# Folding the quadrants of softmax row sums on GpSimd instead of with a matmul

## The chip, the cores and the metric

The kernel runs on one core of a Trainium2 chip. The metric is the time of one execution in device microseconds. Three to eleven executions of a kernel are timed, beside executions of the kernel before on the same chip; those of one kernel agree within some 0.5%. The engines are PE (TensorE matmul), PEld (its weight loads), DVE (VectorE), ACT (ScalarE), POOL (GpSimd) and SP (the engine that issues most DMAs).

## The reference, cut to what matters

Two independent problems A and B of the same shape are solved, and the results are concatenated. The softmax's denominator is the sum over 512 keys for each query and head.

```python
B, Sq, D = 16, 32, 1024
Hq, Hkv, Sk, Dh = 32, 4, 512, 128
q = (x @ wq).reshape(B, Sq, Hq, Dh).transpose(0, 2, 1, 3)
scores = einsum("bhqd,bhkd->bhqk", q, repeat(k)) * Dh ** -0.5
p = softmax(scores)
o = einsum("bhqk,bhkd->bhqd", p, repeat(v))
out = o.transpose(0, 2, 1, 3).reshape(B, Sq, Hq * Dh) @ wo
```

## The kernel before

The main part is a sequence of 128 slots. A slot handles one pair of batch and key head, that is 8 query heads of 32 queries. In slot i PE computes the scores of i (4 matmuls of 256 columns), ACT takes the exponential, DVE sums the probabilities (`partial_sums`), and PE computes the values of slot i - 4 (`LAG = GRP`, 4 matmuls of 256 columns). Between these PE runs six or seven "units", each one 512-column matmul of the query or output projections, so that it always has work.

The keys lie on the partitions, so the row sums have to cross partitions. DVE's reduction with a transpose leaves, in each 32-partition quadrant, the sums of that quadrant's keys. Once in four slots the chunks are added on DVE (`chunk_sums`), the four quadrants are added and spread by one float32r matmul with a constant 0/1 matrix (`fold_sums`), and DVE takes the reciprocal. `spread` widens two slots' reciprocals and `normalize` multiplies them onto the values.

```python
fold = const.tile([P, P // QD, QD], FP32R, name="fold")   # 0/1 matrix, filled by four casts
...
def fold_sums(k):
    cs = quad[k]
    sums = quad[k] = psum.tile([P, GRP * REP], FP32, name="sums", tag="sums", bufs=1)
    nc.tensor.matmul(sums[:], lhsT=fold[...], rhs=cs[...], start=True, stop=True)

def reciprocals(k):
    nc.vector.reciprocal(out=rall[:, k, :], in_=quad.pop(k)[:])
...
ob[j] = psum.tile([P, 2, QW], FP32, name="ob", tag="ob", bufs=1)   # values of two slots, ONE buffer
...
total_slots = 2 * NG                      # 128
LAG = GRP                                 # 4
for i in range(total_slots + LAG):
    live = i < total_slots
    k, o = divmod(i, GRP)
    j, odd = divmod(i - LAG, 2)
    folds = k >= 1 and k <= total_slots // GRP
    if live:
        do_loads(i)
        scores(i)
    run(units, 1)
    if o == 0 and folds:
        chunk_sums(k - 1)
    if i >= LAG:
        values(i - LAG)
    if o == 1 and folds:
        reciprocals(k - 1)
        spread(2 * k - 2)
    if o == 3 and folds:
        spread(2 * k - 1)
    if odd and j >= 0:
        normalize(j)
    run(units, 5)
    if o == 0 and folds:
        fold_sums(k - 1)
    if live:
        partial_sums(i)
    run(units, 1 - (i % 4 == 3))
```

Of the kernel before, what the change touches and what calls it, by code (L numbers as in the profile page):

```python
# [8 lines left out]
BF16 = mybir.dt.bfloat16  # L9
FP32 = mybir.dt.float32  # L10
FP32R = mybir.dt.float32r
I32 = mybir.dt.int32
ACTF = mybir.ActivationFunctionType
ALU = mybir.AluOpType
AX = mybir.AxisListType

P = 128
# [3 lines left out]
REP = HQ // HKV  # L21
QD = 32
# [151 lines left out]
def kernel(  # L174
# [14 lines left out]
    nc = tc.nc  # L189
    B, SQ, D = A_x.shape  # L190
# [3 lines left out]
    KC = SK // P  # L194
    TT = NTOK // P
    NOUT = D
    NW = 512
    NH = NOUT // NW
    GRP = 4
    NG = B * HKV  # L200
    BPT = P // SQ
    QW = REP * SQ
# [7 lines left out]
    def fast_path(ok_i):  # L210
        with ExitStack() as fctx:
            enter = fctx.enter_context
            const = enter(tc.tile_pool(name="const", bufs=1))
            blk = enter(tc.tile_pool(name="blk", bufs=20))
            kv = enter(tc.tile_pool(name="kv", bufs=3))
            work = enter(tc.tile_pool(name="work", bufs=2))
            outp = enter(tc.tile_pool(name="outp", bufs=2))
            psum = enter(tc.tile_pool(name="psum", bufs=2, space=bass.MemoryType.PSUM))
# [7 lines left out]
            nc.scalar.preload_act_table_set("natural_log_exp_and_others")  # L226


            warm = work.tile([P, NW], BF16, name="warm", tag="p_sb", bufs=6)
            nc.vector.memset(warm[:], 0.0)  # L230
            ident = const.tile([P, P], BF16, name="ident")
            make_identity(nc, ident[:])
            fold = const.tile([P, P // QD, QD], FP32R, name="fold")
            for r in range(P // QD):
                rs = slice(r * QD, (r + 1) * QD)
                nc.vector.tensor_copy(
                    out=fold[rs],
                    in_=ident[rs, rs].unsqueeze(1).to_broadcast([QD, P // QD, QD]),
                )
            one_col = const.tile([P, 1], FP32, name="one_col")  # L240
            nc.vector.memset(one_col[:], 1.0)
            shift = const.tile([P, 1], FP32, name="shift")
# [105 lines left out]
            def run(units, n):  # L348
                for _ in range(n):
                    next(units, None)  # L350


            def where(i):
                pr, ii = divmod(i, NG)
                if pr == 0:
                    g, b = divmod(ii, B)
                else:
                    b, g = divmod(ii, HKV)
                return pr, b, g
# [3 lines left out]
            def scores(i):  # L363
                pr, b, g = where(i)
                kT = k_tiles[i // GRP].rearrange("p q (k c) -> p q c k", c=KC)
                s_ps = psum.tile([P, KC, QW], FP32, name="s_ps", tag="s")
                for c in range(KC):
                    nc.tensor.matmul(  # L368
                        s_ps[:, c, :],
                        lhsT=kT[:, i % GRP, c, :],  # L370
                        rhs=qT[pr, g][:, b, :, :].rearrange("p h s -> p (h s)"),
                        start=True,
                        stop=True,
                    )
                p_sb = work.tile([P, KC, QW], BF16, name="p_sb", bufs=6)
                nc.scalar.activation(  # L376
                    out=p_sb[:], in_=s_ps[:], func=ACTF.Exp, bias=shift[:], scale=SCALE
                )
                st[i] = {"p": p_sb}

            parts, rcp, quad = {}, {}, {}

            def partial_sums(i):
                k, q = divmod(i, GRP)
                if q == 0:
                    parts[k] = work.tile([P, GRP, KC, REP], FP32, name="parts", bufs=1)
                nc.vector.tensor_reduce(  # L387
                    out=parts[k][:, q, :, :].rearrange("p c h -> p (c h)"),
                    in_=st[i]["p"][:].rearrange("p c (h s) -> p (c h) s", s=SQ),
                    axis=AX.X, op=ALU.add, apply_transpose=True,  # L390
                )

            def chunk_sums(k):
                cs = quad[k] = work.tile([P, GRP, REP], FP32R, name="cs", bufs=1)
                with nc.allow_low_precision(reason="float32r holds the float32 sum"):
                    nc.vector.tensor_reduce(  # L396
                        out=cs[:], in_=parts.pop(k)[:].rearrange("p q c h -> p q h c"),
                        axis=AX.X, op=ALU.add,
                    )

            def fold_sums(k):
                cs = quad[k]
                sums = quad[k] = psum.tile([P, GRP * REP], FP32, name="sums", tag="sums", bufs=1)
                nc.tensor.matmul(  # L404
                    sums[:],
                    lhsT=fold[:].rearrange("p r s -> p (r s)"),
                    rhs=cs[:].rearrange("p q h -> p (q h)"),
                    start=True,
                    stop=True,
                )  # L410

            def reciprocals(k):
                nc.vector.reciprocal(out=rall[:, k, :], in_=quad.pop(k)[:])  # L413

            def spread(j):
                k, o = divmod(j, 2)
                r = rcp[j] = work.tile([P, 2 * REP, SQ], FP32, name="r")
                nc.vector.transpose(  # L418
                    out=r[:].rearrange("p n s -> p (n s)"),
                    in_=rall[:, k, o * 2 * REP:(o + 1) * 2 * REP]  # L420
                    .unsqueeze(2).to_broadcast([P, 2 * REP, SQ]),
                )
# [3 lines left out]
            def values(i):  # L426
                v_sb = v_tiles[i // GRP]
                j, q = divmod(i, 2)
                if q == 0:
                    ob[j] = psum.tile([P, 2, QW], FP32, name="ob", tag="ob", bufs=1)  # L430
                for c in range(KC):
                    nc.tensor.matmul(  # L432
                        ob[j][:, q, :],
                        lhsT=v_sb[:, i % GRP, c, :],
                        rhs=st[i]["p"][:, c, :],
                        start=(c == 0),
                        stop=(c == KC - 1),
                    )

            def normalize(j):  # L440
                for i in (2 * j, 2 * j + 1):
                    normalized.add(where(i))
                    st.pop(i)
                pr, b, g = where(2 * j)
                tt, bl = divmod(b, BPT)
                if (pr, tt) not in oT:
                    oT[pr, tt] = blk_tile([P, HQ, P], "oT")
                if pr == 0:
                    out = oT[pr, tt][:, g * REP:(g + 1) * REP, bl * SQ:(bl + 2) * SQ]
                    out = out.rearrange("p h (q s) -> p q h s", s=SQ)  # L450
                else:
                    out = oT[pr, tt][:, g * REP:(g + 2) * REP, bl * SQ:(bl + 1) * SQ]
                    out = out.rearrange("p (q h) s -> p q h s", h=REP)
                nc.vector.tensor_tensor(  # L454
                    out=out,
                    in0=rcp.pop(j)[:].rearrange("p (q h) s -> p q h s", h=REP),
                    in1=ob.pop(j)[:].rearrange("p q (h s) -> p q h s", s=SQ),
                    op=ALU.mult,
                )
# [79 lines left out]
            for h, copy in enumerate((nc.vector.tensor_copy, nc.scalar.copy)):  # L539
                copy(  # L540
                    out=qT[0, 0][:, :, h, :],
                    in_=first_q[h][:].rearrange("p (b s) -> p b s", s=SQ),
# [44 lines left out]
            def do_loads(i):  # L587
                for fn, args in plan.get(i, []):
                    fn(*args)


            total_slots = 2 * NG
            LAG = GRP
            for i in range(total_slots + LAG):
                live = i < total_slots
                k, o = divmod(i, GRP)
# [5 lines that stand above are left out]
                run(units, 1)  # L602
                if o == 0 and folds:
                    chunk_sums(k - 1)
                if i >= LAG:
                    values(i - LAG)
                if o == 1 and folds:
# [4 lines that stand above are left out]
                if odd and j >= 0:  # L612
                    normalize(j)
                run(units, 5)
                if o == 0 and folds:
                    fold_sums(k - 1)
                if live:
                    partial_sums(i)
                run(units, 1 - (i % 4 == 3))
# [5 lines left out]
            for k, (lim, op) in enumerate(((1.0 / SUM_HI, ALU.is_ge), (1.0 / SUM_LO, ALU.is_le))):  # L625
                nc.vector.tensor_scalar(
                    out=sq[:], in0=rall[0:QD].rearrange("p j n -> p (j n)"),
# [48 lines left out]
```

## Time and profile before

| before | |
|---|---|
| time, median of 3 | 348.47 us |
| span of the profiled execution | 346.7 us |
| busy PE / DVE / ACT / POOL | 98% / 77% / 54% / 3% |
| chain that ended last | PE 98% |

From the page of the kernel before, part 1 (busy time and share of each engine) and two lines of part 5 (groups: line, engine, operation, output<-inputs, count, then busy us, mean ns of one, and the idle time in front with what ended it):

```profile
PE 341.1 (98%) x2185; PEld 218.4 (63%) x2185; DVE 265.8 (77%) x340; ACT 188.9 (54%) x213; POOL 8.9 (3%) x21
...
L404 PE MATMUL sums<-cs,fold 128*128 128x32 f32 x32 | 11.7, 367 | 0.0
L413 DVE RECIPROCAL rall<-sums 128x32 f32<-128x32 f32 x32 | 10.3, 320 | 0.5 <-PE sums L404 0.5
```

PE is the limit, and the other engines work in its shadow. The fold group, L404, looks like 11.7 us of PE. It is not: the spans of matmuls overlap. The 512-column ones of L312 have a mean span of 379 ns, and six of them below start within 72.25 - 70.96 = 1.29 us, 215 ns apart. The honest price is the distance between starts. The timeline of PE alone (columns: start us, us, engine, line, operation) shows a slot with a fold and the slot after it without one; a slot begins with its score matmuls `s_ps`:

```profile
67.44 0.60 PE L368 MATMUL s_ps<-qT,kT 128*128 128x256 bf16 x4
...
68.53 1.24 PE L312 MATMUL q_ps<-xT,wq_sb 128*128 128x512 bf16 x5
69.42 0.37 PE L404 MATMUL sums<-cs,fold 128*128 128x32 f32 x1
69.64 0.39 PE L312 MATMUL q_ps<-xT,wq_sb 128*128 128x512 bf16 x1
69.87 0.60 PE L368 MATMUL s_ps<-qT,kT 128*128 128x256 bf16 x4
...
70.96 1.46 PE L312 MATMUL q_ps<-xT,wq_sb 128*128 128x512 bf16 x6
72.25 0.60 PE L368 MATMUL s_ps<-qT,kT 128*128 128x256 bf16 x4
```

Both slots hold the same eight 256-column matmuls and seven 512-column ones. The one with the fold takes 69.87 - 67.44 = 2.43 us, the other 72.25 - 69.87 = 2.38 us. So a fold costs about 0.05 us in its place between wide matmuls.

### The profile page before, as it was taken

The page shows a single profiled execution, that of the slowest core. Times are in us where ns is not written, and L with a number is a line of the kernel's source. Part 1 is how long each engine was busy: PE and PEld are TensorE (multiplying, and loading weights), DVE is VectorE, ACT ScalarE, POOL GpSimd, SP SyncE. Part 2 cuts the span into 40 slices and gives each one's busy share as a digit, 9 for nine tenths or more (in the row PEclk, how much of TensorE's full clock was granted, in tenths as well). Part 3 has the DMA queues.
Part 4 walks back from the last instruction along what each step waited for, and adds up shares of the span by engine and source line. Part 5 has one row for each costly group of instructions (what it writes and reads, how often), then busy time and mean ns, then how long its engine had stood idle before and what let it go on. Part 6 is the DMA issues. An engine that isn't in the chain of part 4 may idle for free.

```text
span 346.7 us, 5462 instructions
## 1 busy us (share of the span) xinstructions
PE 341.1 (98%) x2185; PEld 218.4 (63%) x2185; DVE 265.8 (77%) x340; ACT 188.9 (54%) x213; POOL 8.9 (3%) x21
## 2 busy tenths in 40 slices
PE   8999999999999999999999999999999999999995
PEld 5656666666666666666666666666666666666554
DVE  2117888888888888888888888888988888888610
ACT  2357666666666766666655445555455545555000
POOL 0000000000000000000000000000000000000010
PEclk9999999999999999999999999999999999999998
DMA  7999999999986989999998449995669984410000
GB/s 226 247 311 338 164 274 277 242 256 275 247 242 166 209 238 223 297 274 267 278 310 207 110 125 288 351 257 121 137 196 286 301 200 118 112 36 2 15 33 19
DMA packets 125068, 71.70 MB, mean 207 GB/s; under 512 B 73616, under 2 KB 124048, under 8 KB 125040
## 3 DMA queue, kind: packets, MB, share of 16 engines
q1 hardware_dynamic: 124176, 69.29, 80.0%
q0 software_dynamic: 720, 1.97, 1.6%
q8 instruction: 18, 0.29, 0.3%
q14 instruction: 10, 0.08, 0.1%
q10 hardware_dynamic: 144, 0.07, 0.1%
HBM read 51.38 MB, written 2.10 MB: 154 GB/s over the span
## 4 chain that ended last, share of the span: by engine, by line
PE 98%; ACT 0%; issue 0%; DVE 0%; DVEq 0%; ACTq 0%
PE f_ps L331 32%; PE q_ps L312 31%; PE s_ps L368 16%; PE ob L432 16%; PE q_ps L517 1%; PE warm_ps L492 1%; PE xT_ps L507 1%; PE sums L404 0%; ACT o_sb L340 0%; DVE warm L230 0%; PE ok_ps L634 0%; DVEq L671 0%; ACTq L340 0%
## 5 line engine op out<-in xcount | busy, mean ns | idle before, releaser
L376 ACT ACTIVATE p_sb<-s_ps,shift 128x1024 bf16<-128x1024 f32 x128 | 142.5, 1114 | 101.7 <-PE s_ps L368 81.4
L387 DVE TRANSPOSE_TENSOR_REDUCE parts<-p_sb 128x32 f32<-128x1024 bf16 x128 | 158.9, 1241 | 45.5 <-ACT p_sb L376 45.4
L331 PE MATMUL f_ps<-wo_sb,oT 128*128 128x512 bf16 (+1 forms) x544 | 132.5, 367 | 0.0
L312 PE MATMUL q_ps<-xT,wq_sb 128*128 128x512 bf16 x496 | 128.8, 379 | 0.0
L368 PE MATMUL s_ps<-qT,kT 128*128 128x256 bf16 x512 | 76.8, 273 | 0.0
L432 PE MATMUL ob<-p_sb,v_sb 128*128 128x256 bf16 x512 | 76.8, 273 | 0.0
L331 PEld LDWEIGHTS <-oT 128*128 128x128 bf16 x544 | 53.0, 98 | 34.8
L368 PEld LDWEIGHTS <-kT 128*128 128x128 bf16 x512 | 56.9, 113 | 24.7
L312 PEld LDWEIGHTS <-wq_sb 128*128 128x128 bf16 x496 | 48.5, 98 | 35.8 <-DMA wq_sb<-in_A_wq_dram 0.2
L432 PEld LDWEIGHTS <-v_sb 128*128 128x128 bf16 x512 | 50.1, 98 | 19.9
L454 DVE TENSOR_TENSOR oT<-r,ob 128x512 bf16<-128x512 f32 x64 | 44.0, 687 | 8.8 <-PE ob L432 2.3
L320 ACT CAST qT<-q_ps 128x512 bf16<-128x512 f32 x62 | 36.1, 583 | 21.2 <-PE q_ps L312 20.0
L418 DVE STREAM_TRANSPOSE r<-rall 128x512 f32<-128x512 f32 x64 | 44.2, 691 | 1.1
L340 ACT CAST o_sb<-f_ps 128x512 bf16<-128x512 f32 (+1 forms) x17 | 9.5, 558 | 23.2 <-PE f_ps L331 15.2
L342 POOL DMA_DIRECT2D out_dram<-o_sb x15 | 8.2, 549 | 327.3 <-ACT o_sb L340 327.3
L396 DVE TENSOR_REDUCE cs<-parts 128x32 fp32r<-128x128 f32 x32 | 12.1, 377 | 1.1
L404 PE MATMUL sums<-cs,fold 128*128 128x32 f32 x32 | 11.7, 367 | 0.0
L413 DVE RECIPROCAL rall<-sums 128x32 f32<-128x32 f32 x32 | 10.3, 320 | 0.5 <-PE sums L404 0.5
L404 PEld LDWEIGHTS sums<-cs,fold 128*128 128x128 f32 x32 | 6.1, 190 | 3.8
L510 DVE COPY xT<-xT_ps 128x512 bf16<-128x512 bf16 x4 | 1.7, 424 | 5.4 <-PE xT_ps L507 5.4
L510 ACT COPY xT<-xT_ps 128x512 bf16<-128x512 bf16 x4 | 2.2, 587 | 5.6 <-PE xT_ps L507 5.6
L492 PE MATMUL warm_ps<-warm 128*128 128x512 bf16 x7 | 3.4, 630 | 1.3 <-DVE warm L230 1.3
(26 smaller groups left out, 22.2 us busy)
## 6 DMA issues: line engine op xcount, KB each, us to landing
v_sb<-in_A_v_cache_dram SPq DMA_DIRECT2D x16, 512.0 KB, 4.6
wq_sb<-in_B_wq_dram SPq DMA_DIRECT2D x8, 1024.0 KB, 6.2
wo_sb<-in_A_wo_dram SPq DMA_DIRECT2D x8, 1024.0 KB, 6.8
v_sb<-in_B_v_cache_dram SPq DMA_DIRECT2D x16, 512.0 KB, 4.2
wo_sb<-in_B_wo_dram SPq DMA_DIRECT2D x8, 1024.0 KB, 8.9
wq_sb<-in_A_wq_dram SPq DMA_DIRECT2D x7, 1024.0 KB, 7.3
out_dram<-o_sb POOLq DMA_DIRECT2D x15, 128.0 KB, 2.1
x_sb<-in_A_x_dram SPq DMA_DIRECT2D x4, 256.0 KB, 4.1
```

What stands on the lines that cost most here:

```text
L312: nc.tensor.matmul(ps[:], lhsT=w[:, dc, (h % 4) * DH:(h % 4 + 1) * DH], rhs=xT[pr][:, dc, :], start=(dc == 0), stop=(dc == DC - 1),)
L320: nc.scalar.copy(out=qT[pr, g][:, :, hl, :], in_=ps[:].rearrange("p (b s) -> p b s", s=SQ),)
L331: nc.tensor.matmul(ps[:, 0:width], lhsT=oT[pr, tt][:, h, :], rhs=wo_tiles[pr, nh, h // REP][:, h % REP, off:off + width], start=(h == 0), ...
L368: nc.tensor.matmul(s_ps[:, c, :], lhsT=kT[:, i % GRP, c, :], rhs=qT[pr, g][:, b, :, :].rearrange("p h s -> p (h s)"), start=True, stop=True,)
L376: nc.scalar.activation(out=p_sb[:], in_=s_ps[:], func=ACTF.Exp, bias=shift[:], scale=SCALE)
L387: nc.vector.tensor_reduce(out=parts[k][:, q, :, :].rearrange("p c h -> p (c h)"), in_=st[i]["p"][:].rearrange("p c (h s) -> p (c h) s", s=SQ),
L396: nc.vector.tensor_reduce(out=cs[:], in_=parts.pop(k)[:].rearrange("p q c h -> p q h c"), axis=AX.X, op=ALU.add,)
L404: nc.tensor.matmul(sums[:], lhsT=fold[:].rearrange("p r s -> p (r s)"), rhs=cs[:].rearrange("p q h -> p (q h)"), start=True, stop=True,)
L413: nc.vector.reciprocal(out=rall[:, k, :], in_=quad.pop(k)[:])
L418: nc.vector.transpose(out=r[:].rearrange("p n s -> p (n s)"), in_=rall[:, k, o * 2 * REP:(o + 1) * 2 * REP] .unsqueeze(2).to_broadcast([P, ...
L432: nc.tensor.matmul(ob[j][:, q, :], lhsT=v_sb[:, i % GRP, c, :], rhs=st[i]["p"][:, c, :], start=(c == 0), stop=(c == KC - 1),)
L454: nc.vector.tensor_tensor(out=out, in0=rcp.pop(j)[:].rearrange("p (q h) s -> p q h s", h=REP), in1=ob.pop(j)[:].rearrange("p q (h s) -> p ...
```

## The change

The intent is to take the fold off the engine that limits the kernel, and to do it on GpSimd, which is idle for 97% of the span. There it is written as copies and additions: the upper half of the partitions is copied onto the lower and added, the same is done with the second quadrant, and the result is copied back out: six instructions of 32 elements a partition, each waiting for the one before. To give the longer chain time, the values run five slots behind in place of four. That needs a seventh probability buffer, and one of the two spread buffers (each of 2 KB a partition) is given up for it.

```diff
-            fold = const.tile([P, P // QD, QD], FP32R, name="fold")     # and its four casts
...
-                p_sb = work.tile([P, KC, QW], BF16, name="p_sb", bufs=6)
+                p_sb = work.tile([P, KC, QW], BF16, name="p_sb", bufs=7)
...
             def fold_sums(k):
                 cs = quad[k]
-                sums = quad[k] = psum.tile([P, GRP * REP], FP32, name="sums", tag="sums", bufs=1)
-                nc.tensor.matmul(sums[:], lhsT=fold[...], rhs=cs[...], start=True, stop=True)
+                half = work.tile([P, GRP * REP], FP32, name="half", bufs=1)
+                sums = quad[k] = work.tile([P, GRP * REP], FP32, name="sums", bufs=1)
+                flat = cs[:].rearrange("p q h -> p (q h)")
+                nc.gpsimd.tensor_copy(out=half[0:2 * QD], in_=flat[2 * QD:P])
+                nc.gpsimd.tensor_tensor(out=half[0:2 * QD], in0=half[0:2 * QD], in1=flat[0:2 * QD], op=ALU.add)
+                nc.gpsimd.tensor_copy(out=sums[0:QD], in_=half[QD:2 * QD])
+                nc.gpsimd.tensor_tensor(out=sums[0:QD], in0=sums[0:QD], in1=half[0:QD], op=ALU.add)
+                nc.gpsimd.tensor_copy(out=sums[QD:2 * QD], in_=sums[0:QD])
+                nc.gpsimd.tensor_copy(out=sums[2 * QD:P], in_=sums[0:2 * QD])
...
-                r = rcp[j] = work.tile([P, 2 * REP, SQ], FP32, name="r")
+                r = rcp[j] = work.tile([P, 2 * REP, SQ], FP32, name="r", bufs=1)
...
-            LAG = GRP
+            LAG = GRP + 1
...
                 if o == 0 and folds:
                     chunk_sums(k - 1)
+                    fold_sums(k - 1)
...
-                if o == 0 and folds:
-                    fold_sums(k - 1)
```

More of the change, by code (lines that the diff above doesn't have):

```diff
@@ L226, in fast_path @@
             nc.scalar.preload_act_table_set("natural_log_exp_and_others")
-            warm = work.tile([P, NW], BF16, name="warm", tag="p_sb", bufs=6)
+            warm = work.tile([P, NW], BF16, name="warm", tag="p_sb", bufs=7)
             nc.vector.memset(warm[:], 0.0)
@@ L232, in fast_path @@
             make_identity(nc, ident[:])
-            fold = const.tile([P, P // QD, QD], FP32R, name="fold")
-            for r in range(P // QD):
-                rs = slice(r * QD, (r + 1) * QD)
-                nc.vector.tensor_copy(
-                    out=fold[rs],
-                    in_=ident[rs, rs].unsqueeze(1).to_broadcast([QD, P // QD, QD]),
-                )
             one_col = const.tile([P, 1], FP32, name="one_col")
@@ L393, in chunk_sums @@
             def chunk_sums(k):
-                cs = quad[k] = work.tile([P, GRP, REP], FP32R, name="cs", bufs=1)
-                with nc.allow_low_precision(reason="float32r holds the float32 sum"):
-                    nc.vector.tensor_reduce(
-                        out=cs[:], in_=parts.pop(k)[:].rearrange("p q c h -> p q h c"),
-                        axis=AX.X, op=ALU.add,
-                    )
+                cs = quad[k] = work.tile([P, GRP, REP], FP32, name="cs", bufs=1)
+                nc.vector.tensor_reduce(
+                    out=cs[:], in_=parts.pop(k)[:].rearrange("p q c h -> p q h c"),
+                    axis=AX.X, op=ALU.add,
+                )
             def fold_sums(k):
                 cs = quad[k]
-                sums = quad[k] = psum.tile([P, GRP * REP], FP32, name="sums", tag="sums", bufs=1)
-                nc.tensor.matmul(
-                    sums[:],
-                    lhsT=fold[:].rearrange("p r s -> p (r s)"),
-                    rhs=cs[:].rearrange("p q h -> p (q h)"),
-                    start=True,
-                    stop=True,
-                )
+                half = work.tile([P, GRP * REP], FP32, name="half", bufs=1)
+                sums = quad[k] = work.tile([P, GRP * REP], FP32, name="sums", bufs=1)
+                flat = cs[:].rearrange("p q h -> p (q h)")
+                nc.gpsimd.tensor_copy(out=half[0:2 * QD], in_=flat[2 * QD:P])
+                nc.gpsimd.tensor_tensor(
+                    out=half[0:2 * QD], in0=half[0:2 * QD], in1=flat[0:2 * QD], op=ALU.add
+                )
+                nc.gpsimd.tensor_copy(out=sums[0:QD], in_=half[QD:2 * QD])
+                nc.gpsimd.tensor_tensor(
+                    out=sums[0:QD], in0=sums[0:QD], in1=half[0:QD], op=ALU.add
+                )
+                nc.gpsimd.tensor_copy(out=sums[QD:2 * QD], in_=sums[0:QD])
+                nc.gpsimd.tensor_copy(out=sums[2 * QD:P], in_=sums[0:2 * QD])
             def reciprocals(k):
```

## The prediction

> **What bounds the kernel now.** TensorE. The page has PE busy 341.1 of 346.7 us (98%), the chain of waits is 98% PE, the granted clock is 0.997, and in the groups no matmul of the main part has idle time before it. VectorE (77%), ScalarE (54%) and GpSimd (3%) run in PE's shadow. So only what changes PE's own stream, or makes PE wait, moves the time.
>
> **What leaves PE.** 32 fold matmuls (128x32, fp32r) and their weight loads. The groups price them at 11.7 us (367 ns each) plus 6.1 us of loads, but these are overlapping spans: the Trainium skill ("Perfetto Trace Analysis", section "Tensor Engine Instruction") says that PE's end times are estimated, and the trace agrees. I price a fold by the timeline's start-to-start cadence instead. The first score matmuls of successive slots start at 151.71, 154.14, 156.52, 158.91, 161.07 us: a slot of seven 512-column matmuls takes 2.38 us without a fold, 2.43 us with it. At 67.44, 69.87, 72.25, 74.64 us it is the same. One fold costs PE 0.05 us; 32 x 0.05 = 1.6 us (0.46%). That is the whole direct gain, a seventh of the group's busy time. The four casts that build the fold matrix (0.9 us of DVE) ran while DVE waited for PE at the start, and are worth nothing.
>
> **What is added.** 192 GpSimd instructions of 32 elements, each waiting for the one before. The trace has GpSimd memsets of 0.10 to 0.20 us and a dependent select 0.28 us after its predecessor's start, so I estimate 0.25 to 0.35 us a step, 1.5 to 2.1 us a fold, some 55 us of GpSimd in all, in its idle time. The reciprocal, now reading SBUF, should stay near 0.32 us.
>
> **Is the longer chain hidden?** By my slot account the chunk sums end 1.0 to 1.2 us into the first slot of four. The reciprocals come after that slot's normalize and partial sums (687 and 1241 ns), about 0.8 us into the next, so a chain of 2 us costs DVE at most a few tenths. The lag of five moves normalize to even slots. DVE work per slot, from the groups' means, becomes 2.3, 2.25, 1.9, 1.9 us in place of 1.6, 2.95, 1.25, 2.6: all under PE's 2.38 us. The PSUM tile ob has one buffer, so PE waits if normalize is late; I estimate that this begins only when the GpSimd chain is over 3.8 us. At the end 90 instead of 97 output matmuls remain after the loop, the same work in total, and the last normalize is needed 16 matmuls (3.4 us) after its values, so the tail doesn't grow.
>
> **Prediction.** 348.47 - 1.6 = 346.9 us, 8 in 10 between 346.2 and 348.2. Faster by over 2%: 0.01; within 2%: 0.95; slower by over 2%: 0.04.
>
> **What would show it.** Right: no sums matmul on PE; slots of seven at 2.38 us; PE still 98% with next to no waits on DVE; GpSimd 15 to 20% busy; DVE waits for GpSimd before the reciprocal of at most 0.5 us each. Wrong: waits of ob matmuls on oT (normalize), slots longer than 2.38 us, a fold chain above 3.8 us.
>
> **What would make it wrong.** GpSimd steps of 0.6 us or more, whether from their own overhead or from sharing SBUF with VectorE: PE then stalls on ob once in four slots, and 0.3 us each would be 10 us. A late weight load in the first slots, which are 0.4 us shorter in the new order. Or a fold that cost more or less than the cadence shows.

## The result, and the profile after

| | before | after |
|---|---|---|
| time, median | 348.57 us (4 runs) | 347.48 us (4 runs) |
| ratio, 95% interval | | 0.9968, 0.995 to 0.9985 |
| span of the profiled execution | 346.7 us | 345.2 us |

A ratio here is the mean time of one kernel's runs over that of the other's of the same rounds, so it is not quite the ratio of the medians quoted. The time fell by 0.3%, 1.1 us where 1.6 us were predicted; the predicted 346.9 us is 0.6 us under the median, and the median lies in the range.

The page of the changed kernel, part 1 and lines of part 5. The fold group has gone from PE, GpSimd has its six small groups, and the reciprocal waits 1.9 us in all:

```profile
PE 338.6 (98%) x2153; PEld 214.2 (62%) x2153; DVE 264.7 (77%) x336; ACT 188.8 (55%) x213; POOL 50.5 (15%) x213
...
L398 POOL COPY half<-cs 64x32 f32<-64x32 f32 x32 | 6.5, 203 | 206.9 <-DVE cs L388 206.7
...
L410 DVE RECIPROCAL rall<-sums 128x32 f32<-128x32 f32 x32 | 10.2, 317 | 1.9 <-POOL sums L407 1.9
L399 POOL TENSOR_TENSOR half<-half,cs 64x32 f32<-64x32 f32 x32 | 7.7, 242 | 2.6
```

The timeline of PE for the same place, that is the first slot of four and the one after it:

```profile
66.64 0.60 PE L361 MATMUL s_ps<-qT,kT 128*128 128x256 bf16 x4
67.07 0.38 PE L305 MATMUL q_ps<-xT,wq_sb 128*128 128x512 bf16 x1
67.29 0.60 PE L429 MATMUL ob<-p_sb,v_sb 128*128 128x256 bf16 x4
67.73 1.46 PE L305 MATMUL q_ps<-xT,wq_sb 128*128 128x512 bf16 x6
69.02 0.60 PE L361 MATMUL s_ps<-qT,kT 128*128 128x256 bf16 x4
```

The first slot takes 69.02 - 66.64 = 2.38 us, like the slots of seven 512-column matmuls without a fold before. And the timeline of DVE and GpSimd in that slot (ACT and PE lines left out) shows the chain beside DVE's own work:

```profile
67.53 0.38 DVE L388 TENSOR_REDUCE cs<-parts 128x32 f32<-128x128 f32 x1
...
67.93 0.69 DVE L451 TENSOR_TENSOR oT<-r,ob 128x512 bf16<-128x512 f32 x1
67.97 0.20 POOL L398 COPY half<-cs 64x32 f32<-64x32 f32 x1 [7.68 <-DVE cs L388]
68.26 0.24 POOL L399 TENSOR_TENSOR half<-half,cs 64x32 f32<-64x32 f32 x1
68.53 1.24 DVE L380 TRANSPOSE_TENSOR_REDUCE parts<-p_sb 128x32 f32<-128x1024 bf16 x1
...
69.41 0.20 POOL L407 COPY sums<-sums 64x32 f32<-64x32 f32 x1
...
69.69 0.31 DVE L410 RECIPROCAL rall<-sums 128x32 f32<-128x32 f32 x1
```

The chain runs from 67.97 to 69.61 us, 1.64 us, while DVE normalizes and reduces. DVE comes to the reciprocal at 69.69 us without having waited. A step starts 0.26 to 0.31 us after the one before, though the spans are only 0.20 to 0.24 us. The Trainium skill ("Perfetto Trace Analysis", section "GPSIMD Engine Instruction") advises timing GpSimd by start-to-start spacing, not by reported spans; the trace agrees, for the six mean spans sum to 1.29 us only.

The Trainium skill ("GPSIMD Engine Reference", section "Key points") warns that GpSimd shares SBUF interfaces with VectorE, with contention for DVE instructions in a two-port mode or with two SBUF inputs. No cost of that kind shows here: the partial sums, the spread and the normalize have means of 1241, 691 and 687 ns in both pages' groups, with GpSimd at 3% and at 15%, and the normalize and the partial sums that run beside the chain above take 0.69 and 1.24 us like the rest. It is no test of the warning, though: each of these instructions has at most one input in SBUF (the normalize reads `ob` from PSUM), and no run here shows whether one of them uses a two-port mode.

### The profile page after: what moved, and what is told of

Same layout as the page of the kernel before. It is cut to its first block, busy times and chain, and to the rows that moved or that the text cites. A ratio compares the mean times of both kernels' runs of the same rounds, so it can differ in the third digit from the quotient of the medians.

```text
span 345.2 us, 5555 instructions
## 1 busy us (share of the span) xinstructions
PE 338.6 (98%) x2153; PEld 214.2 (62%) x2153; DVE 264.7 (77%) x336; ACT 188.8 (55%) x213; POOL 50.5 (15%) x213
## 4 chain that ended last, share of the span: by engine, by line
PE 97%; DMA 1%; SPq 0%; ACT 0%; issue 0%; ACTq 0%
PE f_ps L324 32%; PE q_ps L305 31%; PE s_ps L361 16%; PE ob L429 16%; DMA wq_sb<-in_A_wq_dram 1%; PE q_ps L514 1%; PE xT_ps L504 0%; SPq L466 0%; ACT o_sb L333 0%; PE ok_ps L630 0%; SPq L667 0%; ACTq L333 0%
## 5 line engine op out<-in xcount | busy, mean ns | idle before, releaser
L380 DVE TRANSPOSE_TENSOR_REDUCE parts<-p_sb 128x32 f32<-128x1024 bf16 x128 | 158.8, 1241 | 30.7 <-ACT p_sb L369 29.0
L398 POOL COPY half<-cs 64x32 f32<-64x32 f32 x32 | 6.5, 203 | 206.9 <-DVE cs L388 206.7
L388 DVE TENSOR_REDUCE cs<-parts 128x32 f32<-128x128 f32 x32 | 12.1, 377 | 1.1
L410 DVE RECIPROCAL rall<-sums 128x32 f32<-128x32 f32 x32 | 10.2, 317 | 1.9 <-POOL sums L407 1.9
L399 POOL TENSOR_TENSOR half<-half,cs 64x32 f32<-64x32 f32 x32 | 7.7, 242 | 2.6
L403 POOL TENSOR_TENSOR sums<-sums,half 32x32 f32<-32x32 f32 x32 | 7.7, 241 | 2.6
L407 POOL COPY sums<-sums 64x32 f32<-64x32 f32 x32 | 6.6, 205 | 1.9
L406 POOL COPY sums<-sums 32x32 f32<-32x32 f32 x32 | 6.4, 201 | 2.0
```

What stands on the lines that cost most here:

```text
L380: nc.vector.tensor_reduce(out=parts[k][:, q, :, :].rearrange("p c h -> p (c h)"), in_=st[i]["p"][:].rearrange("p c (h s) -> p (c h) s", s=SQ),
L388: nc.vector.tensor_reduce(out=cs[:], in_=parts.pop(k)[:].rearrange("p q c h -> p q h c"), axis=AX.X, op=ALU.add,)
```

## The experiments

The theory, A: the gain is the PE time of 32 folds, and everything else is hidden. The rivals: B, the gain comes from the better balanced DVE order that the lag brings; C, the fold is worth more on PE, and the GpSimd chain takes a part back.

One number tells the kernels apart better than the total time. A four-slot period is the distance between the first score matmuls of slots i and i + 4, its median taken over the steady part of a profiled execution. And the stretch from the first score matmul to the issue of the last output leaves out the start, where PE waits for the first loads (22.1 to 23.0 us in these executions), and the landing of the last output (1.6 to 2.4 us), which both scatter. All kernels together:

| kernel | four-slot period us | first scores to last output issue us | last output lands in us | ratio to before |
|---|---|---|---|---|
| before | 9.36 | 342.85 - 22.41 = 320.44 | 1.6 | 1 |
| changed | 9.32 | 341.29 - 22.22 = 319.07 | 1.7 | 0.9968 |
| changed, again | 9.32 | 341.71 - 22.63 = 319.08 | 2.0 | 0.9959 |
| changed, third | 9.32 | 341.74 - 22.66 = 319.08 | 2.0 | 0.9974 |
| lag only | 9.36 | 343.59 - 23.02 = 320.57 | 1.6 | 1.0004 |
| no fold | 9.32 | 342.11 - 23.03 = 319.08 | 1.8 | 0.9965 |
| no lag | 9.32 | 342.54 - 22.30 = 320.24 | 2.4 | 1.0 |
| no lag, filled | 9.32 | 342.14 - 22.92 = 319.22 | 2.4 | 0.9991 |
| no lag, filled, again | 9.32 | 341.33 - 22.14 = 319.19 | 2.1 | 0.9974 |
| four folds | 9.51 | 347.53 - 22.48 = 325.05 | 1.7 | 1.0148 |

The two ends of the stretch in the timelines, first of the kernel before and then of the changed one (all between left out):

```profile
22.41 0.60 PE L368 MATMUL s_ps<-qT,kT 128*128 128x256 bf16 x4
...
342.85 0.38 ACTq L342 DMA_DIRECT2D out_dram<-o_sb  x1
```

```profile
22.22 0.60 PE L361 MATMUL s_ps<-qT,kT 128*128 128x256 bf16 x4
...
341.29 0.38 ACTq L335 DMA_DIRECT2D out_dram<-o_sb  x1
```

### 1. The changed kernel again

No edit.

> The changed kernel once more, unedited, for a narrower interval. Theory A (the gain is the PE time of 32 fold matmuls, 0.05 us each): 1.4 to 1.6 us faster than before, ratio 0.9955 to 0.996. Rival B (the gain comes from the better balanced VectorE order that the lag brings) and rival C (the fold is worth more on PE, and the GpSimd chain takes some of it back) expect the same of this run; it is the yardstick for the other three.

Measured: 347.36 us against 348.73 us, ratio 0.9959 (0.9946 to 0.9972). A third time, with experiment 9:

> The changed kernel once more on the same chip as the filled version, as its yardstick: ratio 0.9955 to 0.997 against before.

Measured: 347.74 us against 348.6 us, ratio 0.9974 (0.9962 to 0.9987). The three ratios average 0.9967, about 1.15 us. The gain is real and small.

### 2. The lag alone

```diff
-bufs=6                                       # p_sb, kernel before
+bufs=7
-name="r")
+name="r", bufs=1)
-LAG = GRP
+LAG = GRP + 1
```

> The kernel before with the lag of five, seven probability buffers and one spread buffer, the fold still a matmul. Theory A: no gain, ratio 0.999 to 1.001, slots with a fold still at 2.43 us. Rival B: most of the gain is here, ratio about 0.996.

Measured: 348.98 us against 348.73 us, ratio 1.0004 (0.9991 to 1.0018), period 9.36 us. Rival B falls: the new DVE order alone brings nothing, because DVE was not what PE waited for.

### 3. No fold at all, wrong result on purpose

```diff
             def fold_sums(k):                # kernel before
-                (the matmul)
+                pass
-                cs = ... FP32R
+                cs = ... FP32                # the reciprocals read cs
```

> Wrong result on purpose: the kernel before with the fold matmul left out and the reciprocals taken of the unfolded sums, lag of four, nothing on GpSimd. The bound of what taking the fold off PE can give. Theory A: the same as the changed kernel within 0.1%, ratio 0.9955 to 0.996. Rival C: clearly faster than the changed kernel, ratio 0.993 or less.

Measured: 347.59 us against 348.73 us, ratio 0.9965 (0.9952 to 0.9977); the result is wrong, as meant. Its stretch of 319.08 us is that of the changed kernel to 0.01 us. So the GpSimd chain costs PE nothing, and the changed kernel has all there is to be had from this. Rival C falls.

### 4. Four folds in place of one

Three further fold matmuls, one in each other slot, write unused columns of the same PSUM tile.

```diff
-                    fold_sums(k - 1)
+                    fold_sums(k - 1)         # kernel before, now into sums[:, 0, :]
+                if o > 0 and folds:
+                    fold_into(k - 1, o)      # the same matmul into sums[:, o, :]
```

> The kernel before with the fold matmul issued in each slot of four instead of in one (three extra ones go to other columns of the same PSUM tile and are not used): 96 more fold matmuls on PE. Theory A (0.05 us each): plus 4.8 us, ratio 1.014; somewhat more if the one in front of the short score matmuls hides its weight load less well. If the group's busy time (367 ns) were the price: plus 35 us, ratio 1.10.

Measured: 353.62 us against 348.47 us, ratio 1.0148 (1.0131 to 1.0165). The period rose from 9.363 to 9.509 us, 0.049 us for each added fold; the stretch rose by 4.61 us, 0.048 us for each of 96. The group's line in this run's answer by groups still says 367 ns for each:

```profile
L412 PE MATMUL sums<-cs,fold 128*128 128x32 f32 x128 | 47.0, 367 | 0.0
```

So 35.3 us more of "busy" cost 5.2 us of time. The start-to-start price is right and the span is off by a factor of seven. Theory A stands.

### 5. GpSimd's fold without the lag

```diff
-bufs=7                                       # p_sb, changed kernel
+bufs=6
-name="r", bufs=1)
+name="r")
-LAG = GRP + 1
+LAG = GRP
```

> The changed kernel with the lag of four, six probability buffers and two spread buffers again; the fold stays on GpSimd. Theory A with a chain of 1.7 us that still fits behind VectorE's own work (I count 0.4 us of slack left in VectorE's loop): as the changed kernel, ratio 0.9955 to 0.997, no waits of PE. Rival B: no gain, about 1.0. If the lag is needed to hide the chain: slower than before, ratio over 1.0, with PE waiting on the normalize.

Measured: 348.72 us against 348.73 us, ratio 1.0 (0.9988 to 1.0012). None of the expectations fits as a whole. By the time alone it is what rival B foretold, but the period is 9.32 us, that of the changed kernel, where B would have 9.36 us. The trace shows where the gain went. In the last four rounds of the loop there are no scores, and a round is only 1.95 us long. The timeline of this run's end (PE weight loads and some other lines left out):

```profile
321.13 0.60 PE L429 MATMUL ob<-p_sb,v_sb 128*128 128x256 bf16 x4
...
321.56 1.67 PE L324 MATMUL f_ps<-wo_sb,oT 128*128 128x512 bf16 x7
...
321.90 0.21 POOL L407 COPY sums<-sums 64x32 f32<-64x32 f32 x1
322.14 0.35 DVE L410 RECIPROCAL rall<-sums 128x32 f32<-128x32 f32 x1 [1.75 <-POOL sums L407]
323.34 0.69 DVE L451 TENSOR_TENSOR oT<-r,ob 128x512 bf16<-128x512 f32 x1
...
324.09 0.61 PE L429 MATMUL ob<-p_sb,v_sb 128*128 128x256 bf16 x4 [0.85 <-DVE oT L451]
```

The product at 324.09 us needs the single `ob` buffer, which the normalize at 323.34 us frees, which needs the reciprocal, which waited 1.75 us for GpSimd. From 321.13 to 324.09 us is 2.96 us, where the usual round is 1.95 us: 1.0 us lost once, of a gain of 1.37 us. Two single periods of 9.39 and 9.40 us took 0.14 us more, so the stretch is still 0.2 us under before; in the time of the profiled execution the landing of 2.4 us, against 1.6 us, hides that. In the changed kernel the reciprocal waits at the same place too, 1.15 us, but the lag has put a round between it and the product:

```profile
321.32 0.35 DVE L410 RECIPROCAL rall<-sums 128x32 f32<-128x32 f32 x1 [1.15 <-POOL sums L407]
...
322.41 0.60 PE L429 MATMUL ob<-p_sb,v_sb 128*128 128x256 bf16 x4
...
323.05 0.69 DVE L451 TENSOR_TENSOR oT<-r,ob 128x512 bf16<-128x512 f32 x1 [0.63 <-PE ob L429]
...
324.36 0.60 PE L429 MATMUL ob<-p_sb,v_sb 128*128 128x256 bf16 x4
```

### 6. to 8. A longer chain on GpSimd

Pairs of full copies between `half` and `sums` are added to the end of the chain, in all ten, twelve and eighteen steps in place of six.

```diff
+                for _ in range(2):           # 3 and 6 for twelve and eighteen steps
+                    nc.gpsimd.tensor_copy(out=half[:], in_=sums[:])
+                    nc.gpsimd.tensor_copy(out=sums[:], in_=half[:])
```

> The changed kernel with four more GpSimd copies in the fold chain, ten steps, about 2.8 us. VectorE runs in order, so chunk sums, chain, reciprocal and the rest of four slots close a loop, which I count from the start-to-start times of the changed kernel's trace as 8.2 us against PE's 9.35 us: 1.15 us of slack, enough for four steps. Loop theory: as the changed kernel, ratio 0.996 to 0.998. The prediction's threshold of 3.8 us: as the changed kernel too.

> The changed kernel with six more GpSimd copies, twelve steps, about 3.3 us. Loop theory: the loop is 0.5 us over PE's four slots, so plus 16 us, ratio about 1.04. The prediction's threshold of 3.8 us: still hidden, ratio 0.996.

> The changed kernel with twelve more GpSimd copies, eighteen steps, about 5 us. Loop theory: plus 67 us (2.15 us for each of 31 loops), ratio about 1.19. The prediction's threshold of 3.8 us: 1.2 us for each of 31, plus 37 us, ratio 1.10.

| steps | period us | time us (before 348.47) | ratio, 95% interval |
|---|---|---|---|
| 6 | 9.32 | | |
| 10 | 9.32 | 347.89 | 0.9985 (0.9969 to 1.0002) |
| 12 | 9.53 | 355.58 | 1.0208 (1.0191 to 1.0225) |
| 18 | 11.17 | 409.21 | 1.173 (1.1705 to 1.1756) |

The ten-step run has no stall in its period, and its stretch is 341.61 - 22.34 = 319.27 us, 0.2 us over the changed kernel's; its ratio is less good than that, without a cause that I can name. Above the threshold six steps add 11.167 - 9.530 = 1.637 us, 0.273 us each, one for one with the chain, whose added copies start 0.27 us apart: a loop. Ten steps (a chain of 2.74 us) cost PE nothing in the period and twelve (3.28 us) cost 0.21 us, so the limit lies between. Going back along the slope, the period leaves 9.321 us at 11.2 steps, by estimate a chain of 1.64 + 5.2 x 0.273 = 3.06 us. That is not the prediction's 3.8 us. The timeline of the eighteen-step run shows the loop from one chunk sum to the next:

```profile
64.75 0.37 DVE L388 TENSOR_REDUCE cs<-parts 128x32 f32<-128x128 f32 x1
...
66.43 1.11 ACT L369 ACTIVATE p_sb<-s_ps,shift 128x1024 bf16<-128x1024 f32 x1 [1.22 <-PE s_ps L361]
...
70.21 0.35 DVE L413 RECIPROCAL rall<-sums 128x32 f32<-128x32 f32 x1 [3.34 <-POOL sums L410]
...
71.23 1.20 DVE L380 TRANSPOSE_TENSOR_REDUCE parts<-p_sb 128x32 f32<-128x1024 bf16 x1
...
73.06 0.60 PE L432 MATMUL ob<-p_sb,v_sb 128*128 128x256 bf16 x4 [1.68 <-DVE oT L454]
...
75.91 0.38 DVE L388 TENSOR_REDUCE cs<-parts 128x32 f32<-128x128 f32 x1
```

DVE keeps the order of its program: the probabilities that are ready at 66.43 + 1.11 = 67.54 us are summed only at 71.23 us, after the reciprocal that waited for GpSimd. From chunk sum to reciprocal are 5.46 us, from there to the next chunk sum 5.70 us of DVE work without a wait. With six steps the first part is 69.69 - 67.53 = 2.16 us, so the loop is 2.16 + 5.70 = 7.86 us, an estimate, and 9.32 - 7.86 = 1.46 us are free. My count before the run, 8.2 us, was of starts in the changed kernel, where DVE has waits between its instructions; where it has none, they follow each other up to 0.13 us more closely (from spread to partial sums 0.76 us there, 0.63 us here). So twelve steps cost less than I expected (355.58 us, 7.1 us over before, for some 16), and eighteen too (60.7 us for 67). The prediction looked at one pass only: it asked when a late reciprocal would make the normalize late. It missed that the next chunk sums wait behind the same late work, so that lateness adds up from round to round until PE stalls.

### 9. Without the lag, and the end filled

Five output matmuls that ran after the loop are put in front of the product that waited in experiment 5.

```diff
-                run(units, 1)
+                run(units, 6 if i == total_slots + 2 else 1)
```

> The run without the lag kept the shorter four-slot period (9.32 us) in its trace but lost about 1.0 us once, at the end, where a slot without scores is only 1.95 us and the first of the last two value products waited for the normalize before it. Here five output matmuls that ran after the loop are put in front of that product, nothing else changes. End theory: the wait is filled, time as the changed kernel, 1.2 to 1.5 us under before, ratio 0.9955 to 0.9965. If the lag is needed in the steady part: about 1.0 again.

Measured: 348.48 us against 348.6 us, ratio 0.9991 (0.9978 to 1.0004): by the time alone, a miss. The trace says that the wait is filled. PE's timeline of the end has no gap in front of the product at 324.77 us:

```profile
322.18 2.75 PE L324 MATMUL f_ps<-wo_sb,oT 128*128 128x512 bf16 x12
324.77 0.60 PE L429 MATMUL ob<-p_sb,v_sb 128*128 128x256 bf16 x4
```

The stretch to the last issue is 319.22 us, 1.22 us under before. But the last output took 2.4 us to land in the profiled execution. So it was run again, unedited:

> The filled version without the lag, once more, unedited. Its first run was 0.9991 of before although its PE work from the first score matmul to the last output issue was 1.22 us shorter (319.22 against 320.44 us): the last output took 2.4 us to land in the profiled execution, against 1.6 us in before and 1.7 to 2.0 us in the changed kernel. If that landing time is chance: 1.6 to 2.0 us here and a ratio of 0.996 to 0.9975. If it belongs to this kernel: 2.4 us again and 0.998 to 1.0.

Measured: 347.73 us against 348.69 us, ratio 0.9974 (0.9959 to 0.9989), stretch 319.19 us, landing 2.1 us. The end theory stands on the traces of both runs; of the times, the second shows a gain and the first does not, and both are less than the 0.9955 to 0.9965 expected at first. The landing of 2.1 us falls between the two expectations, so what sets the landing time of the last output stays open: 1.6 us in before, in the lag alone and in the run of experiment 10, 1.7 to 2.4 us in all others, one profiled execution each.

### 10. Twelve steps without the lag

The two edits of experiments 5 and 7 together.

> Twelve GpSimd steps with the lag of four. With the lag of five one normalize of VectorE runs beside the chain; with four both lie in VectorE's loop, about 0.6 us more. The run of twelve steps with the lag had a period of 9.53 us. Loop theory: about 10.1 to 10.2 us, plus 25 us against before, ratio 1.07. If the lag bought nothing in the loop: 9.53 us, ratio 1.02.

Measured: 394.17 us against 348.6 us, ratio 1.1312 (1.1296 to 1.1329), period 10.67 us. The direction is right and the size is not: without the lag the same chain costs far more, 10.67 against 9.53 us, and more than the 10.2 us that I counted from DVE alone. This run's timeline shows the loop:

```profile
67.19 0.35 DVE L413 RECIPROCAL rall<-sums 128x32 f32<-128x32 f32 x1 [1.75 <-POOL sums L410]
...
68.39 0.69 DVE L454 TENSOR_TENSOR oT<-r,ob 128x512 bf16<-128x512 f32 x1
...
69.13 0.60 PE L432 MATMUL ob<-p_sb,v_sb 128*128 128x256 bf16 x4 [1.19 <-DVE oT L454]
...
72.15 0.69 DVE L454 TENSOR_TENSOR oT<-r,ob 128x512 bf16<-128x512 f32 x1 [0.20 <-PE ob L432]
...
74.03 0.37 DVE L388 TENSOR_REDUCE cs<-parts 128x32 f32<-128x128 f32 x1
```

The late normalize (68.39 us) stalls PE, and the next normalize (72.15 us) then waits for the delayed PE in turn. From the reciprocal to the next chunk sum are 74.03 - 67.19 = 6.84 us, against 5.70 us with the lag. Of these 1.14 us some 0.65 us are the second normalize in the loop, from start to start. Some 0.45 us more pass because both normalizes, which read the spread just before them, start later after it than the partial sums do with the lag; 0.20 us of that is the wait for PE. So the lag is worth about 1.1 us of room in the loop, which the chain of six steps does not need (2.13 + 6.84 = 8.97 us, an estimate, against 9.32 us), and a round's distance at the end, which it does.

No version beat the changed kernel. The filled one without the lag comes within 0.15 us of it in the stretch; that its time is equal is not shown (ratios of 0.9991 and 0.9974, against 0.9959 to 0.9974).

## Why the prediction was right or wrong

- **PE is the limit, and the fold is worth its cadence, not its busy time: right.** The stretch shrank by 1.37 us, 0.043 us for each of 32 folds; the period says 9.363 - 9.321 = 0.042 us. The prediction's 0.05 us came from starts rounded to 0.01 us and was a little high, so 1.6 us were really 1.4 us. The added folds of experiment 4 cost 0.048 us.
- **The rest of the difference** between 1.37 us and the 1.15 us of the timed runs lies outside the stretch, in the first loads and the landing of the last output. Whether the changed kernel's landing of 1.7 to 2.0 us against 1.6 us is its own doing was not settled. Of the four casts that the change drops nothing is to be seen: the first scores start at 22.22, 22.63 and 22.66 us without them, at 22.41 us (before) and 23.02 us (lag alone) with them.
- **The GpSimd chain: right.** Predicted 1.5 to 2.1 us a fold, measured 1.64 us; GpSimd at 15%. The reciprocal stayed at 317 ns.
- **Hidden: right, with one detail off.** PE does not wait on DVE in the changed kernel. The waits of the reciprocal were to be at most 0.5 us each; there are three, 0.48, 0.23 and 1.15 us, the longest in the short rounds at the end.
- **The threshold of 3.8 us: wrong.** The step that failed is "I estimate that this begins only when the GpSimd chain is over 3.8 us". It begins between 2.74 and 3.28 us, by estimate at 3.06 us, because DVE's in-order work closes a loop with the chain. The error had no effect at 1.64 us.
- **The tail doesn't grow: right, but only with the lag.** The prediction took the tail from the number of matmuls left and from the 16 matmuls between the last values and the need for their normalize; it does not speak of the short rounds before them. Experiment 5 shows that the same chain with a lag of four loses 1.0 us there, most of the gain.

## What to carry to other kernels

Price an instruction on a saturated TensorE by the start-to-start distance of what surrounds it, with and without it: here the busy time of a narrow matmul overstated its worth by a factor of seven to nine. When a small step goes to an idle engine, ask for two limits: whether the in-order engine behind it closes a loop that still fits the period, and whether the last rounds, which are shorter, still hide it. Where a gain of a few tenths of a per cent disappears, compare the steady period and the ends of the traces separately before giving up the idea.

## What the Trainium skill lacked or had wrong

- "TensorE: Matmul & The Clock Gate", section "Back-to-back issue gap", gives about 131 ns as the sustained spacing of 512-column matmuls with weight loads, and says that the single-matmul formula of about 216 ns over-counts. In this kernel six of them, each with its own weight load, take 72.25 - 70.96 = 1.29 us, 215 ns each, on a PE without waits. The formula fits, and the sustained figure does not.
- The same section gives about 25 ns for a matmul of 1 to 64 columns, as an isolated gap that leaves out the weight load. No page gives the cost of a 128x32 float32r matmul between wide bf16 ones: 0.042 to 0.049 us here, with a profiled span of 367 ns.
- "GPSIMD Engine Reference", section "Elementwise — side-by-side cycle accounting", gives a time for 2048 elements (4497 ns for an add) and no figure for small instructions or their fixed cost. Here a 32-element float32 copy has a span of 0.20 us and an add 0.24 us, and a dependent step follows after 0.26 to 0.31 us.
- "DMA: Bandwidth & Descriptors", section "Anatomy of one DMA — SWDGE (gpsimd) path", gives a fixed cost of about 2 us for a DMA, as nearly constant. No page says how far one and the same transfer scatters from run to run: the last 64 KB output, issued from ACT, landed in 1.6 to 2.4 us here, a scatter of 0.8 us where the effect under study is 1.15 us.
